# Grouped-query attention decode with token mixing: chunks of 4 MB in a ring of two, no V chunk kept over the layers, four V tiles in one matmul

## The chip, the cores and the metric

The kernel runs on one core of one Trainium2 chip. The metric is the device time of one execution in microseconds, as the median of several runs. Before the change it is 2613.38 us (3 runs, 2611.53 to 2614.95).

## What is computed

Two layers, each an attention block over a cached K and V and then a small MLP over the token axis. There are 2 sequences (B) with one new token each, 32 query heads on 8 K/V heads, 32768 cached positions (Sk) and heads of 128 (Dh). All is float32. Both layers read the same caches and weights. K and V hold 268 MB each, so two layers read 1074 MB of them.

```python
def _A_ref(x, k_cache, v_cache, wq, wo):
    q = (x @ wq).reshape(B, Sq, Hq, Dh).transpose(0, 2, 1, 3)
    k = jnp.repeat(k_cache, rep, axis=1)
    v = jnp.repeat(v_cache, rep, axis=1)
    scores = jnp.einsum("bhqd,bhkd->bhqk", q, k) * (Dh ** -0.5)
    p = _softmax(scores, axis=-1)
    o = jnp.einsum("bhqk,bhkd->bhqd", p, v)
    return o.transpose(0, 2, 1, 3).reshape(B, Sq, Hq * Dh) @ wo
...
def _B_ref(x, w1, b1, w2, b2):
    h = _layernorm(x, axis=-1)
    u = jnp.einsum("bsd,sf->bdf", h, w1) + b1
    u = _gelu(u)
    y = jnp.einsum("bdf,fs->bds", u, w2) + b2
    return y.transpose(0, 2, 1)
...
x = x + _A_ref(_layernorm(x, axis=-1), A_k_cache, A_v_cache, A_wq, A_wo)
x = x + _B_ref(_layernorm(x, axis=-1), B_w1, B_b1, B_w2, B_b2)
x = x + _A_ref(_layernorm(x, axis=-1), A_k_cache, A_v_cache, A_wq, A_wo)
x = x + _B_ref(_layernorm(x, axis=-1), B_w1, B_b1, B_w2, B_b2)
```

## The kernel before

The work is cut into 32 units: 2 layers times 2 sequences times 8 K/V heads. A unit has 8 K chunks and 8 V chunks (`NCH`) of 4096 positions (`CK`), 2 MB each: 128 rows of 16 KB. The host lays K out transposed, so that a chunk has Dh on the partitions; a V chunk has 32 positions on each partition, one V tile (`j`) of 128 columns for each of them.

All chunks go through one ring of three tiles (`chunk`, L53, L168 and L237), and all their DMAs are issued on SyncE's queue (SP), in the order of the program. A DMA into a ring tile waits until the matmuls that read the tile's last content are done. The first V chunk of the last K/V head is different: with `KEEP` = 1 it is loaded once into a tile of its own (L233) and used in both layers.

`k_chunk` (L165) multiplies the chunk by the four queries of the group. `qpad` has the queries in a window of zeros, so that each matmul adds its scores in other rows of the same PSUM tile: 128 x 32 stationary, 512 columns moving, on one of four column groups of TensorE (`g`). `SUB` windows for each chunk and `PACK` chunks fill one PSUM tile; VectorE then transposes it by blocks into `S` (L189) and takes maxima (L190). `max_1` and `max_2` (L199, L207) bring the maximum of the unit to all partitions, and ScalarE takes the exponentials and their sums (L217).

`v_chunk` (L228) multiplies each V tile by its four columns of `S`, one matmul of 128 columns each, into one PSUM accumulator, four rows in each of four column groups. `out_1` (L257) copies the accumulator, adds the groups up with a selection matrix (`selg`) and divides by the sum; `out_2` (L268) multiplies by wo. After the last head of a sequence comes the mixer: `mix_2` (layer norms), `mix_3` (VectorE and GELU on ScalarE, in four pieces of 2, 4, 4 and 4 tiles of 512), `mix_3_out` (TensorE) and `mix_4`. In the very last mixer, the pieces of `mix_3` use ring tiles (L301).

The order of the work on each engine is that of the program (`manual_schedule`). A list of slots (L343 to L393) sets it: in slot s the K chunk s is issued and multiplied, then come the `pre` steps, then V chunk s - NCH - LAG, then the `post` steps. The small steps of a unit (`make_q`, the loads of wq and wo, `max_1`, `out_1` and the mixer) are put in slots by hand. The last V chunk of the kernel is loaded in pieces of 16, 8, 4 and 4 tiles (`PIECES`).

Of the kernel before, what the change touches and what calls it, by code (L numbers as in the profile page):

```python
# [8 lines left out]
F32 = mybir.dt.float32  # L9
# [4 lines left out]
P = 128  # L14
CK = 4096
JT = CK // P
NG = 4
SUB = 2
PACK = 4
RING = 3  # L20
LAG = 1
KEEP = 1
PIECES = (16, 8, 4, 4)
GELU_GROUPS = (2, 4, 4, 4)
# [4 lines left out]
def gqa_mixer_kernel(ctx: ExitStack, tc: tile.TileContext, x, kt, v, wq, wo, cols, out):  # L29
# [19 lines left out]
    SCALE = DH ** -0.5  # L49
    assert DH == P and R * PACK * SUB == 32 and DT == NG and R == NG and D == 512  # L50

# [20 lines left out]
    def load_wo(h):  # L72
# [16 lines left out]

    selg = const.tile([P, R], F32, name="selg")  # L90
    nc.vector.tensor_reduce(
        selg, ident.rearrange("p (g r) -> p r g", g=NG)[:, :R, :], axis=AX.X, op=ALU.add
    )
# [6 lines left out]
    for t in acc:  # L100
        nc.vector.memset(t[:, :DH], 0.0)
    rows = pfix.tile([P, 512], F32, name="rows")
# [125 lines left out]
    def v_chunk(n, c):  # L228
# [14 lines left out]
        half, i = divmod(c, PACK)  # L243
        a = acc[n % 2]
        for j in range(JT):
            g = j % NG
            k, jj = divmod(j, JT // SUB)
            col = jj * 32 + (SUB * i + k) * R
            nc.tensor.matmul(  # L249
                a[32 * g : 32 * g + R, :DH],  # L250
                S[n][:, half, col : col + R],
                vc[:, j * DH : (j + 1) * DH],
                start=(c == 0 and j < NG),
                stop=(c == NCH - 1 and j >= JT - NG),
            )

    def out_1(n):  # L257
        asb = work.tile([P, DH], F32, name="asb", bufs=1)
        nc.vector.tensor_copy(asb, acc[n % 2][:, :DH])
        po = pmisc.tile([P, 512], F32, name="misc")  # L260
        nc.tensor.matmul(po[:, R : 2 * R], ones, lsum[n], start=True, stop=True)  # L261
        nc.tensor.matmul(po[:, :R], asb, selg, start=True, stop=True)  # L262
# [85 lines left out]
    for n in range(NU):  # L348
        layer, b, h = unit_of(n)
        s0 = n * NCH  # L350
        if n:
            at(post, s0 - 4, make_q, n, 0)
            at(pre, s0 - 3, make_q, n, 1)
            at(post, s0 - 3, make_q, n, 2)
            at(pre, s0 - 2, make_q, n, 3)
        if n and n < HKV:
            at(post, s0 - 6, load_wq, h)
        if n < HKV:
            at(post, s0 + NCH + 2, load_wo, h)
        at(pre, s0 + NCH, max_1, n)  # L360
        at(post, s0 + NCH, max_2, n)
        e = s0 + 2 * NCH + LAG
        at(pre, e, out_1, n)
        at(post, e, out_2, n)
        if h == HKV - 1:
            key = (layer, b)
            at(post, e, take_rows, key)
            at(pre, e + 1, mix_2, key)
            for k, w in enumerate(GELU_GROUPS):
                at(pre, e + 2 + k, mix_3, key, sum(GELU_GROUPS[:k]), w)  # L370
                at(post, e + 2 + k, mix_3_out, key, sum(GELU_GROUPS[:k]), w)
            at(post, e + 5, take_rows, key)
            at(pre, e + 6, mix_4, key)
            if layer + 1 < LAYERS:
                at(pre, e + 7, lambda k: to_columns(k, hx[k]), (layer + 1, b))

# [19 lines left out]
def _layout(A_x, A_k_cache, A_v_cache, A_wq, A_wo, B_w1, B_b1, B_w2, B_b2):  # L396
# [7 lines left out]

    kt = A_k_cache.reshape(B * HKV, n, NG, 32, SUB, JT // SUB, DH).transpose(0, 1, 6, 4, 2, 5, 3)
    wq = A_wq.reshape(D // P, P, HKV, -1).transpose(2, 1, 0, 3)
# [35 lines left out]
```

## Time and profile before

| | |
|---|---|
| median of 3 runs | 2613.38 us |
| the profiled execution, its time | 2613.11 us |
| its span, first to last instruction | 2611.3 us |
| mean granted clock of TensorE | 0.786 |
| HBM read | 1088.45 MB |
| chunk DMAs, K / V, from issue to landing (median) | 11.9 / 12.1 us |

PE is TensorE's matmuls and PEld its weight loads, DVE is VectorE, ACT ScalarE, POOL GpSimd. SP is SyncE; SPq is its queue, on which it issues DMAs. In the rows of the timeline stand start and duration in us, engine, line and operation, the tiles written and read, the number of instructions taken together, and in brackets the idle time before them and what ended it. In the rows of groups, the count is followed by busy time in us, the mean of one in ns, and the idle time before them with its cause. In the rows of stretches stand, after the length, busy time and count for PE, PEld, DVE, ACT and POOL, then the granted clock of TensorE (1.00 is full speed), the busy share of the DMA engines and GB/s. The queues' rows give packets, MB and the share of the time of 16 DMA engines.

### The profile page before, as it was taken

Reading aid. Unit: us, or ns where it says so; the run is one execution under the profiler, and the core shown is the slowest. Engines: PE = TensorE matmul, PEld = TensorE weight load, DVE = VectorE, ACT = ScalarE, POOL = GpSimd, SP = SyncE. Lnnn points to the kernel's source line nnn. Section 1 sums busy time; section 2 is a strip of 40 time slices with the busy share of each in tenths; the row PEclk is TensorE's granted clock in tenths of the full one; section 3 lists DMA queues with packets and bytes.
Section 4 is the critical chain, followed back from the end, with each engine's and each line's share of the span. In section 5 each row is a group of like instructions: output and inputs, shape, how many; then the busy total and the mean of one; then the engine's idle time right before and its main releaser. Section 6 shows DMA issues by size and latency. Waiting matters only on the chain.

```text
span 2611.3 us, 46425 instructions
## 1 busy us (share of the span) xinstructions
PE 1640.0 (63%) x22184; PEld 838.7 (32%) x22184; DVE 210.7 (8%) x473; ACT 135.3 (5%) x280; POOL 7.0 (0%) x21
## 2 busy tenths in 40 slices
PE   6556656566566666666666656656657666566665
PEld 3323323233333332332333333333323333233322
DVE  1000000000021000000002000000001100000002
ACT  0000000000010000000001000000000100000001
POOL 0000000000000000000000000000000000000000
PEclk8777777777888787887878888788787877877777
DMA  9999999999999999999999999999999999999995
GB/s 405 426 426 425 419 425 422 424 422 426 420 426 420 425 423 421 424 423 424 426 421 425 422 424 422 423 424 424 420 426 422 424 423 423 424 425 419 426 424 230
DMA packets 76660, 1091.44 MB, mean 418 GB/s; under 512 B 8628, under 2 KB 8628, under 8 KB 9016
## 3 DMA queue, kind: packets, MB, share of 16 engines
q1 hardware_dynamic: 76324, 1088.46, 98.8%
q8 instruction: 173, 2.83, 0.4%
q14 instruction: 15, 0.12, 0.0%
q10 hardware_dynamic: 148, 0.03, 0.0%
HBM read 1088.45 MB, written 0.00 MB: 417 GB/s over the span
## 4 chain that ended last, share of the span: by engine, by line
DMA 79%; PE 19%; issue 1%; DVE 0%; ACT 0%; SPq 0%; POOL 0%; POOLq 0%; DVEq 0%; ACTq 0%
DMA chunk<-in_kt_dram 40%; DMA chunk<-in_v_dram 40%; PE scores L178 9%; PE acc L249 9%; PE misc L153 0%; PE rows L322 0%; DVE chunk L307 0%; PE misc L132 0%; ACT chunk L315 0%; PE bcast L290 0%; ACT S L217 0%; DVE ln_st L110 0%; DVE row L114 0%; PE rows L271 0%; PE bcast L291 0%
## 5 line engine op out<-in xcount | busy, mean ns | idle before, releaser
L249 PE MATMUL acc<-chunk,S 128*4 128x128 f32 x16256 | 702.3, 344 | 478.5 <-DMA chunk<-in_v_dram 477.9
L178 PE MATMUL scores<-chunk,qpad 128*32 128x512 f32 x4096 | 678.8, 795 | 465.4 <-DMA chunk<-in_kt_dram 464.9
L249 PEld LDWEIGHTS acc<-chunk,S 128*4 128x4 f32 x16256 | 499.9, 105 | 767.4 <-DMA chunk<-in_v_dram 605.4
L178 PEld LDWEIGHTS scores<-chunk,qpad 128*32 128x32 f32 x4096 | 132.4, 128 | 783.0 <-DMA chunk<-in_kt_dram 410.5
L217 ACT ACTIVATE S<-S,neg 128x256 f32<-128x256 f32 x128 | 95.3, 749 | 2286.2 <-DVE neg L213 2286.2
L153 PEld LDWEIGHTS misc<-xnT,wq 128*128 128x128 f32 x1024 | 143.3, 217 | 97.3 <-issue 97.3
L153 PE MATMUL misc<-xnT,wq 128*128 128x1 f32 x1024 | 153.8, 272 | 0.0
L189 DVE STREAM_TRANSPOSE S<-scores 128x512 f32<-128x512 f32 x64 | 45.9, 717 | 899.1 <-PE scores L178 899.1
L161 DVE COPY qpad<-misc 128x4 f32<-128x4 f32 x32 | 5.2, 163 | 795.9 <-PE misc L153 795.9
L190 DVE TENSOR_REDUCE mx<-S 128x4 f32<-128x512 f32 x64 | 67.8, 1059 | 2.2
L271 PE MATMUL rows<-wo,oT 128*1 128x512 f32 x256 | 38.8, 679 | 0.5 <-DVE oT L266 0.5
L205 DVE TENSOR_REDUCE m<-misc 4x1 f32<-4x128 f32 x32 | 8.9, 279 | 230.0 <-PE misc L203 230.0
L315 ACT ACTIVATE hid<-hid 128x2048 f32<-128x2048 f32 (+1 forms) x12 | 20.4, 1697 | 130.0 <-DVE hid L307 130.0
L307 DVE TENSOR_SCALAR hid<-row,cols_sb 128x512 f32<-128x512 f32 x42 | 20.2, 542 | 58.6 <-PE rows L322 58.6
L217 ACT ACTIVATION_READ_ACCUMULATOR S<-S,neg 128x1 f32 x128 | 23.9, 187 | 0.0
L261 PEld LDWEIGHTS misc<-lsum,one 128*128 128x128 f32 x64 | 10.9, 214 | 37.0 <-issue 36.9
L264 DVE RECIPROCAL rl<-misc 128x4 f32<-128x4 f32 x32 | 5.9, 183 | 142.8 <-PE misc L262 142.8
L213 DVE TENSOR_SCALAR neg<-misc 128x4 f32<-128x4 f32 x32 | 5.2, 162 | 149.4 <-PE misc L209 149.4
L203 PEld LDWEIGHTS misc<-ident,mxa 128*4 128x4 f32 x64 | 6.4, 102 | 27.5 <-issue 26.6
L322 PE MATMUL rows<-hid,cols_sb 128*1 128x512 f32 x84 | 14.5, 688 | 1.2 <-ACT hid L315 1.2
L203 PE MATMUL misc<-ident,mxa 128*4 128x128 f32 x64 | 14.5, 314 | 0.8 <-DVE mxa L201 0.8
L209 PEld LDWEIGHTS misc<-ident,m 4*128 4x128 f32 x64 | 11.5, 222 | 10.8 <-issue 10.2
(50 smaller groups left out, 189.6 us busy)
## 6 DMA issues: line engine op xcount, KB each, us to landing
chunk<-in_kt_dram SPq DMA_DIRECT2D x256, 2048.0 KB, 11.9
chunk<-in_v_dram SPq DMA_DIRECT2D x253, 2048.0 KB, 12.1
wq<-in_wq_dram SPq DMA_DIRECT2D x8, 1024.0 KB, 16.0
wo<-in_wo_dram SPq DMA_DIRECT2D x8, 1024.0 KB, 13.4
kept<-in_v_dram SPq DMA_DIRECT2D x1, 2048.0 KB, 15.9
chunk<-in_v_dram SPq DMA_DIRECT2D x1, 1024.0 KB
chunk<-in_v_dram SPq DMA_DIRECT2D x1, 512.0 KB, 9.9
chunk<-in_v_dram SPq DMA_DIRECT2D x2, 256.0 KB, 10.2
```

The costliest lines, as they stand in the source:

```text
L153: nc.tensor.matmul(q_ps[n][:, r : r + 1], wq_sb[h][:, d, r * DH : (r + 1) * DH], xnT[layer, b][:, d : d + 1], start=(d == 0), stop=(d == D ...
L178: nc.tensor.matmul(sc_ps[n][32 * g : 32 * g + 32, :], q, kc[:, (k * NG + g) * w : (k * NG + g + 1) * w], start=(i == 0 and k == 0), stop=( ...
L189: nc.vector.transpose(S[n][:, half, :], sc_ps[n])
L190: nc.vector.tensor_reduce(mx[n][:, half, :], S[n][:, half, :].rearrange("p (t h) -> p h t", h=R), axis=AX.X, op=ALU.max,)
L203: nc.tensor.matmul(pm[:R, :P], mxa, ident, start=True, stop=True)
L209: nc.tensor.matmul(pm[:, :R], m4[n].to_broadcast([R, P]), ident[:R, :R], start=True, stop=True)
L217: nc.scalar.activation(s[:, :, h], s[:, :, h], AF.Exp, bias=neg[:, h : h + 1], scale=SCALE, accum_out=lsum[n][:, h : h + 1],)
L249: nc.tensor.matmul(a[32 * g : 32 * g + R, :DH], S[n][:, half, col : col + R], vc[:, j * DH : (j + 1) * DH], start=(c == 0 and j < NG), sto ...
L271: nc.tensor.matmul(rows[32 * r : 32 * r + 1, :], oT[n][:, r : r + 1], wo_sb[h][:, r, :], start=(h == 0), stop=(h == HKV - 1),)
L307: nc.vector.tensor_scalar(u[:, k * D : (k + 1) * D], hx[key], w1c[:, f : f + 1], b1c[:, f : f + 1], op0=ALU.mult, op1=ALU.add,)
L315: nc.scalar.activation(u[:, : n * D], u[:, : n * D], AF.Gelu_apprx_tanh)
L322: nc.tensor.matmul(rows[32 * g : 32 * g + 1, :], w2c[:, f : f + 1], u[:, k * D : (k + 1) * D], start=(f < NG), stop=(f >= FT - NG),)
```

## The change

A chunk is twice as large (8192 positions, 4 MB, rows of 32 KB), the ring has two tiles, and no V chunk is kept. A unit has 4 K and 4 V chunks, so there are half as many slots and the steps in the slots are moved. In `v_chunk` one matmul takes four V tiles: 512 columns moving, and as stationary the 16 columns of `S` that belong to the four tiles. Of its 16 x 512 results only the blocks where tile and columns belong together are used: `out_1` copies the whole accumulator and picks the blocks with four matmuls. The host lays K out so that the 16 columns stand side by side. The last V chunk has one more piece, of 32 tiles, ahead of the others. Each piece of the mixer is put in the slots next to the `mix_3_out` of the piece before it.

```diff
-CK = 4096
+CK = 8192
 JT = CK // P
 NG = 4
-SUB = 2
-PACK = 4
-RING = 3
+SUB = 4
+PACK = 2
+RING = 2
 LAG = 1
-KEEP = 1
-PIECES = (16, 8, 4, 4)
+KEEP = 0
+PIECES = (32, 16, 8, 4, 4)
+QT = 4
...
-    selg = const.tile([P, R], F32, name="selg")
+    selg = const.tile([P, R * QT], F32, name="selg")
...
-        a = acc[n % 2]
-        for j in range(JT):
-            g = j % NG
-            k, jj = divmod(j, JT // SUB)
-            col = jj * 32 + (SUB * i + k) * R
-            nc.tensor.matmul(
-                a[32 * g : 32 * g + R, :DH],
-                S[n][:, half, col : col + R],
-                vc[:, j * DH : (j + 1) * DH],
-                start=(c == 0 and j < NG),
-                stop=(c == NCH - 1 and j >= JT - NG),
-            )
+        w = QT * DH
+        a, c2 = divmod(i, PACK // 2)
+        for q in range(JT // QT):
+            g = q % NG
+            col = (c2 * (JT // QT) + q) * 32 + a * R * QT
+            nc.tensor.matmul(
+                acc[n % 2][32 * g : 32 * g + R * QT, :],
+                S[n][:, half, col : col + R * QT],
+                vc[:, q * w : (q + 1) * w],
+                start=(c == 0 and q < NG),
+                stop=(c == NCH - 1 and q >= JT // QT - NG),
+            )
...
-        asb = work.tile([P, DH], F32, name="asb", bufs=1)
-        nc.vector.tensor_copy(asb, acc[n % 2][:, :DH])
+        asb = work.tile([P, QT * DH], F32, name="asb", bufs=1)
+        nc.vector.tensor_copy(asb, acc[n % 2])
...
-        nc.tensor.matmul(po[:, :R], asb, selg, start=True, stop=True)
+        for t in range(QT):
+            nc.tensor.matmul(
+                po[:, :R],
+                asb[:, t * DH : (t + 1) * DH],
+                selg[:, t * R : (t + 1) * R],
+                start=(t == 0),
+                stop=(t == QT - 1),
+            )
...
-            at(post, s0 - 4, make_q, n, 0)
-            at(pre, s0 - 3, make_q, n, 1)
-            at(post, s0 - 3, make_q, n, 2)
-            at(pre, s0 - 2, make_q, n, 3)
+            at(post, s0 - 3, make_q, n, 0)
+            at(pre, s0 - 2, make_q, n, 1)
+            at(post, s0 - 2, make_q, n, 2)
+            at(pre, s0 - 1, make_q, n, 3)
         if n and n < HKV:
-            at(post, s0 - 6, load_wq, h)
+            at(post, s0 - 4, load_wq, h)
         if n < HKV:
-            at(post, s0 + NCH + 2, load_wo, h)
+            at(post, s0 + NCH + 1, load_wo, h)
...
+            places = [(post, e + 1), (pre, e + 2), (post, e + 2), (pre, e + 3), (post, e + 3)]
             for k, w in enumerate(GELU_GROUPS):
-                at(pre, e + 2 + k, mix_3, key, sum(GELU_GROUPS[:k]), w)
-                at(post, e + 2 + k, mix_3_out, key, sum(GELU_GROUPS[:k]), w)
-            at(post, e + 5, take_rows, key)
-            at(pre, e + 6, mix_4, key)
+                f0 = sum(GELU_GROUPS[:k])
+                at(*places[k], mix_3, key, f0, w)
+                at(*places[k + 1], mix_3_out, key, f0, w)
+            at(post, e + 3, take_rows, key)
+            at(pre, e + 4, mix_4, key)
             if layer + 1 < LAYERS:
-                at(pre, e + 7, lambda k: to_columns(k, hx[k]), (layer + 1, b))
+                at(pre, e + 5, lambda k: to_columns(k, hx[k]), (layer + 1, b))
...
-    kt = A_k_cache.reshape(B * HKV, n, NG, 32, SUB, JT // SUB, DH).transpose(0, 1, 6, 4, 2, 5, 3)
+    kt = A_k_cache.reshape(B * HKV, n // PACK, 2, PACK // 2, NG, 32, JT // QT, QT // SUB, SUB, DH)
+    kt = kt.transpose(0, 1, 2, 7, 9, 8, 4, 3, 6, 5)
```

More of the change, by code (lines that the diff above doesn't have):

```diff
@@ L49, in gqa_mixer_kernel @@
     SCALE = DH ** -0.5
-    assert DH == P and R * PACK * SUB == 32 and DT == NG and R == NG and D == 512
+    assert DH == P and R * PACK * SUB == 32 and PACK * SUB == 2 * QT and DT == NG and R == NG and D == 512
     const = ctx.enter_context(tc.tile_pool(name="const", bufs=1))
@@ L88, in gqa_mixer_kernel @@
     nc.gpsimd.memset(half_neg, -0.5)
-    selg = const.tile([P, R], F32, name="selg")
+    selg = const.tile([P, R * QT], F32, name="selg")
     nc.vector.tensor_reduce(
-        selg, ident.rearrange("p (g r) -> p r g", g=NG)[:, :R, :], axis=AX.X, op=ALU.add
+        selg, ident.rearrange("p (g r) -> p r g", g=NG)[:, : R * QT, :], axis=AX.X, op=ALU.add
     )
@@ L100, in gqa_mixer_kernel @@
     for t in acc:
-        nc.vector.memset(t[:, :DH], 0.0)
+        nc.vector.memset(t, 0.0)
     rows = pfix.tile([P, 512], F32, name="rows")
```

## The prediction

> **What bounds the kernel now.** I read the page of the profile first: busy time by engine, the 40 slices, the queues, the chain that ended last.
>
> ```profile
> span 2611.3 us, 46425 instructions
> PE 1640.0 (63%) x22184; PEld 838.7 (32%) x22184; DVE 210.7 (8%) x473; ACT 135.3 (5%) x280; POOL 7.0 (0%) x21
> DMA  9999999999999999999999999999999999999995
> GB/s 405 426 426 425 419 425 422 424 422 426 420 426 420 425 423 421 424 423 424 426 421 425 422 424 422 423 424 424 420 426 422 424 423 423 424 425 419 426 424 230
> DMA packets 76660, 1091.44 MB, mean 418 GB/s; under 512 B 8628, under 2 KB 8628, under 8 KB 9016
> q1 hardware_dynamic: 76324, 1088.46, 98.8%
> q8 instruction: 173, 2.83, 0.4%
> DMA 79%; PE 19%; issue 1%; DVE 0%; ACT 0%; SPq 0%; POOL 0%; POOLq 0%; DVEq 0%; ACTq 0%
> ```
>
> No compute engine is near full, while the 16 DMA engines are busy in every slice but the last. Slices 2 to 39 average 423.4 GB/s (38 figures of the fifth line), and the best reach 426. So the kernel streams bytes, with a head (405 in the first slice) and a tail (230 in the last). The chain's "PE 19%" need not contradict this, so I looked at the chain in order of time and at the timeline of a quiet stretch.
>
> ```profile
> 842.07 12.68 DMA chunk<-in_v_dram
> 856.78 12.68 DMA chunk<-in_kt_dram
> ```
> ```profile
> 835.17 3.37 PE L249 MATMUL acc<-chunk,S 128*4 128x128 f32 x64 [3.30 <-DMA chunk<-in_v_dram]
> 838.58 0.33 SPq L169 DMA_DIRECT2D chunk<-in_kt_dram  x1
> 840.08 1.92 PE L178 MATMUL scores<-chunk,qpad 128*32 128x512 f32 x16 [1.54 <-DMA chunk<-in_kt_dram]
> 842.07 0.33 SPq L241 DMA_DIRECT2D chunk<-in_v_dram  x1
> ```
>
> One turn of the ring is 856.78 - 842.07 = 14.71 us for three chunks, 4.90 us for 2.097 MB (428 GB/s). Of these 12.68 go from issue to landing and 2.03 on PE. A chunk alone moves in 4.90, so at its issue 12.68 - 4.90 = 7.8 us of older transfers still stood in the queue. PE's time lies under that queue: it is on the chain because a ring closes through PE, but shorter matmuls would only lengthen the wait in the queue.
>
> **The change, part by part.**
>
> *Bytes.* KEEP = 0 loads the last unit's first V chunk in both layers: 2.097 MB more, at 423.4 GB/s +4.95 us. Nothing hides it, since the queue is full.
>
> *Four V tiles in one matmul.* The profile counts two matmuls and two weight loads for each call.
>
> ```profile
> L249 PE MATMUL acc<-chunk,S 128*4 128x128 f32 x16256 | 702.3, 344 | 478.5 <-DMA chunk<-in_v_dram 477.9
> L178 PE MATMUL scores<-chunk,qpad 128*32 128x512 f32 x4096 | 678.8, 795 | 465.4 <-DMA chunk<-in_kt_dram 464.9
> ```
> ```profile
> 2580.93 1.93 PE L249 MATMUL acc<-chunk,S 128*4 128x128 f32 x64 [1.56 <-DMA chunk<-in_v_dram]
> ```
> ```profile
> 40.12 3.62 PE L178 MATMUL scores<-chunk,qpad 128*32 128x512 f32 x16 [1.99 <-DMA chunk<-in_kt_dram]
> ```
> ```profile
> 835.00:840.00 5.00, 3.37 (x64) 2.38 (x64) 0.00 (x0) 0.00 (x0) 0.00 (x0) 0.66 1.01 433
> 840.00:845.00 5.00, 1.94 (x19) 0.43 (x21) 0.00 (x0) 0.00 (x0) 0.00 (x0) 1.00 0.99 423
> ```
>
> A V chunk now is 64 matmuls of 128 columns, later 16 of 512 for the same 2 MB: the same 8192 columns, the form a K chunk has already. At granted clock 1.00 both take 1.92 to 1.93 us, at a lower clock (0.66 over the V burst at 835) 3.37 to 3.62. So PE's time per byte stays, and a 4 MB chunk takes 2 x 1.92 = 3.84 us warm and about 2 x 3.5 = 7.0 slow. What falls is the count: 254 chunks x 64 stand in the row (256 with the two it lacks, 16,384), later 4,096, each with its weight load, so 24,576 instructions go; out_1's three more calls in each of 32 units add 384. That is 24,192 of 46,425, or 52%, and the instruction queue shrinks with them. By bytes, 1.47 MB at 423.4 GB/s is 3.5 us; by its 0.4% of the span (10.4 us), 5.4. I take -4.5, from rows on both sides.
>
> *DMAs of 4 MB.* Some 260 DMAs and half of the small packets go. No row prices a DMA by itself. The bounds are 0 and, if that fixed work is all that keeps the average slice at 423.4 below 426, 0.6% of 2580 = -16 us. I take 0: neighbouring slices of one kernel differ by more (419 beside 425), so the dips are not a cost of each DMA.
>
> *The ring of two.* This is the term that decides.
>
> ```profile
> 1.43 0.62 SPq L65 DMA_DIRECT2D xrow<-in_x_dram  x2
> 3.37 0.69 DVE L110 BATCH_NORM_STATS2 ln_st<-xrow 128x6 f32<-128x512 f32 x1 [0.89 <-DMA xrow<-in_x_dram]
> ```
>
> After a landing, PE works 3.84 to 7.0 us, SP issues (0.04 us behind PE: 835.17 + 3.37, then 838.58), and the transfer starts. The two 2 KB transfers bound that start: 3.37 - 1.43 = 1.9 us at most, landing included. Meanwhile one chunk is under way, 2 x 4.90 = 9.8 us. The margin is 9.8 - 3.84 - 1.9 = 4.1 us warm and 0.9 slow; before, with two chunks of 4.90 behind the landed one, it was 6.0 to 4.3. So a quiet chunk does not run dry. But the margin holds for the slowest of 16 DMA engines, and they need not be level: 173 instruction fetches at 0.4% x 16 x 2611.3 / 173 = 0.97 us each fall on single engines (16 KB in one packet), so an engine can be two fetches, 1.9 us, behind the others. Those in front then wait where the margin is below that. Bounds: 0, and 83 remaining fetches each paid in full, 80 us. The margin covers two to four fetches unless the clock is slow, so I take one in twenty, +4.
>
> The Trainium skill, TensorE: Matmul & The Clock Gate, section Why this matters for your kernels, speaks against the change: a PE pause above about 3 us puts the clock back to half. With bursts 9.8 us apart the pause would be up to 6 us, against 1.5 to 3.3 in the rows above, which already show clocks of 0.66. By that rule every chunk starts slow and the margin lies nearer 0.9 than 4.1; the sum keeps its +4, and the dry ring below gets a higher chance.
>
> *Steps moved between slots.* A slot is now a K and a V chunk of 4 MB, 19.6 us in place of 9.8, so each make_q, max and GELU piece has as much time per chunk as before or more. wq and wo loads stay on SP between chunk issues and wait for nothing. One step collides: out_1 now follows the K chunk whose scores are transposed (an odd chunk with PACK 2), so PE waits there for DVE.
>
> ```profile
> L189 DVE STREAM_TRANSPOSE S<-scores 128x512 f32<-128x512 f32 x64 | 45.9, 717 | 899.1 <-PE scores L178 899.1
> L190 DVE TENSOR_REDUCE mx<-S 128x4 f32<-128x512 f32 x64 | 67.8, 1059 | 2.2
> ```
>
> That is 0.72 + 1.06, then the copy of acc (0.69) and four pairs of 0.39, in all 4.0 us behind K's 3.84 to 7.0, against 9.8 to V's landing. I cost it at nothing: V's transfer is the cover. Slow, it makes V 1.2 us late, 32 x 1.2 = 38 us at most if no margin is left.
>
> *Head and tail.* At the head, the queue holds wq, K, wq, K (10.5 MB, 25 us) while PE does the first chunk: 0. In the tail nothing is hidden.
>
> ```profile
> 2586.18 0.40 PE L249 MATMUL acc<-chunk,S 128*4 128x128 f32 x8 [0.24 <-DMA chunk<-in_v_dram]
> ...
> 2586.65 0.29 DVE L259 COPY asb<-acc 128x128 f32<-128x128 f32 x1 [32.55 <-PE acc L249]
> ...
> 2587.00 0.39 PE L262 MATMUL misc<-selg,asb 128*128 128x4 f32 x2
> ...
> 2588.96 0.69 DVE L283 COPY row<-rows 128x512 f32<-128x512 f32 x1 [1.16 <-PE rows L271]
> ...
> 2601.23 0.10 PEld L322 LDWEIGHTS rows<-chunk,cols_sb 128*1 128x1 f32 x8 [1.71 <-ACT chunk L315]
> 2601.45 1.92 DVE L307 TENSOR_SCALAR chunk<-row,cols_sb 128x512 f32<-128x512 f32 x4 [0.84 <-PE rows L322]
> 2603.03 0.10 PEld L322 LDWEIGHTS rows<-chunk,cols_sb 128*1 128x1 f32 x8 [1.70 <-ACT chunk L315]
> 2603.49 1.91 ACT L315 ACTIVATE chunk<-chunk 128x2048 f32<-128x2048 f32 x1 [0.50 <-DVE chunk L307]
> 2605.45 1.04 PE L322 MATMUL rows<-chunk,cols_sb 128*1 128x512 f32 x8 [1.13 <-ACT chunk L315]
> ...
> 2607.38 1.12 PE L334 MATMUL bcast<-row,selg 128*128 128x512 f32 x2 [0.89 <-DVE row L283]
> ```
>
> The last piece: one call of 512 columns, 1.12 as at L334, for 0.40 (+0.7). The copy of acc: 0.69, as L283 copies 512 columns from PSUM, for 0.29 (+0.4). Three more pairs of 0.39, partly overlapped (+1.0). The last GELU pieces take ring buffers, now two: the third piece must wait for the first one's matmuls, as the fourth did (DVE at 2601.45), so it takes the fourth's place on DVE (to 2603.4) and ACT (to 2605.4), and the fourth ends one ACT pass, 1.9 us, later. In all +4.0; bounds +2 (the matmuls overlap, the pieces do not shift) and +5.
>
> **The sum.** 2611.3 + 4.95 - 4.5 + 0 + 4 + 4.0 = 2619.8 us of span. The profiled run took 2613.1, so 1.8 lie around the span, and it is 0.3 below the median of 2613.38: 2619.8 + 1.8 + 0.3 = 2622 us, 0.3% slower. The terms are small beside the bytes, and of both signs.
>
> **The rivals.**
>
> *Large rows stream faster* (not slower). If the 4 MB DMAs hold every slice at 426 GB/s, the stream loses 16 us: 2622 - 16 = 2606. For it: half as many DMAs, packets and instruction fetches. Against it: 426 is reached today with 16 KB rows, and the dips have no rhythm of chunks. It decides from an average of 425 GB/s upwards, where the stream is 9 us shorter.
>
> The Trainium skill, DMA: Bandwidth & Descriptors, section Anatomy of one DMA, fits a DMA as 2.0 us fixed plus its bytes at 436 GB/s; 256 DMAs fewer would by that be 512 us, an estimate of some 2110. The ring's turn of 14.71 us for three chunks leaves no such gaps, because queued DMAs overlap, and I give that outcome no chance.
>
> *The ring covers all of it.* The lag of DMA engines costs 0 and the tail +4: 2618, 0.17% slower, not told from no change. For it: the margin of 4.1 when warm. Against it: the clocks of 0.66.
>
> *The ring runs dry.* Chunks at half clock leave 0.9 us, and every engine's lag, and every late V behind out_1, goes through to the stream. Price: half of the 80 for the fetches and a quarter of the 38, 40 + 10 = 50 us, 2622 - 4 + 50 = 2668. For it: pauses above those of today. Against it: a burst that starts slow need not end slow (1.93 for a V chunk at 2580.93, behind a pause).
>
> *The change does not do what it says*: PE's 1640 us hardly fall, because the columns stream as before. That holds in each case and costs nothing, as PE is not the bound.
>
> **How the numbers follow.** Forecast 0.45 (2619 to 2632), covered ring 0.22 (2613 to 2618.6), faster stream 0.21, dry ring 0.12. No change means within 0.2%, 2608.2 to 2618.6, about what a measurement of this kernel can tell. Slower: 0.45 + 0.12 = 0.57, plus a little of the edge, 0.58; same 0.22 less the edge, 0.21; faster 0.21. The range reaches from 2604, just beyond the faster case's price, to 2648, half way into the dry ring's 2632 to 2668.
>
> **What would show it.** Right: q8 near 83 packets and 1.4 MB; acc matmuls 4,096 of 512 columns at about the K row's mean; chunk DMAs of 4096 KB landing in 19.6 - 6 = some 13 to 15 us; slices still 421 to 425 GB/s; a tail 4 us longer between the last landing and the end. Wrong: slices at 426 and above throughout (fast rival), or slices under 420 with PE waits of more than the 9.8 us of a transfer (dry ring), or a PE burst of a chunk under 3.8 us. The forecast falls if the mean rate of the middle slices moves by more than 1% either way.

## The result, and the profile after

The changed kernel takes 2689.37 us (median of 4 runs, 2677.4 to 2692.84) against 2613.93 before on the same chip: a ratio of 1.0282, 95% interval 1.0249 to 1.0315. It is slower by 75 us, where the prediction had 2622 and a range of 2604 to 2648. The profiled execution took 2688.18 us, its span is 2686.4.

The page of the changed kernel, the lines that answer to those of before:

```profile
span 2686.4 us, 21703 instructions
PE 1675.4 (62%) x10088; PEld 522.9 (19%) x10088; DVE 219.5 (8%) x473; ACT 133.5 (5%) x280; POOL 7.0 (0%) x21
GB/s 408 420 420 425 413 418 421 421 399 416 402 413 400 417 409 416 405 410 409 413 411 407 405 419 412 404 414 405 411 411 408 409 417 405 413 406 418 404 411 212
DMA packets 39986, 1091.95 MB, mean 406 GB/s; under 512 B 4564, under 2 KB 4564, under 8 KB 4952
q1 hardware_dynamic: 39748, 1090.54, 97.4%
q8 instruction: 79, 1.29, 0.2%
DMA 71%; PE 27%; DVE 1%; issue 0%; ACT 0%; SPq 0%; POOL 0%; POOLq 0%; DVEq 0%; ACTq 0%
L180 PE MATMUL scores<-chunk,qpad 128*32 128x512 f32 x4096 | 699.4, 846 | 509.2 <-DMA chunk<-in_kt_dram 509.2
L253 PE MATMUL acc<-chunk,S 128*16 128x512 f32 x4096 | 712.7, 859 | 399.1 <-DMA chunk<-in_v_dram 399.1
chunk<-in_kt_dram SPq DMA_DIRECT2D x128, 4096.0 KB, 15.0
```

Nothing was added on PE: it is busy 1675 us, where it was 1640, with less than half the matmuls, and the instruction queue fell from 173 packets to 79. What changed is the stream: slices 2 to 39 average 411.5 GB/s (before 423.4), and none of them reaches 426. Nearly the whole loss is there: the 1050 MB of these slices at 411.5 in place of 423.4 take 72 us longer. The stream is lower nearly everywhere (399 to 425), which points at a cause in each turn of the ring and not in a few places. In the chain PE's share rose from 19% to 27%.

The next view is the timeline of the changed kernel in a stretch without a mixer, PE's bursts on a chunk and SP's issues alone:

```profile
1007.54 5.32 PE L253 MATMUL acc<-chunk,S 128*16 128x512 f32 x32 [0.45 <-DMA chunk<-in_v_dram]
1012.92 0.33 SPq L243 DMA_DIRECT2D chunk<-in_v_dram  x1
1017.29 3.64 PE L180 MATMUL scores<-chunk,qpad 128*32 128x512 f32 x32 [2.58 <-DMA chunk<-in_kt_dram]
1020.99 0.33 SPq L171 DMA_DIRECT2D chunk<-in_kt_dram  x1
1027.26 6.29 PE L253 MATMUL acc<-chunk,S 128*16 128x512 f32 x32 [5.34 <-DMA chunk<-in_v_dram]
1033.62 0.33 SPq L243 DMA_DIRECT2D chunk<-in_v_dram  x1
1036.97 6.56 PE L180 MATMUL scores<-chunk,qpad 128*32 128x512 f32 x32 [2.44 <-DMA chunk<-in_kt_dram]
1043.60 0.33 SPq L171 DMA_DIRECT2D chunk<-in_kt_dram  x1
```

Each issue follows its burst at once, and the bursts are long: 5.3, 3.6, 6.3, 6.6 us. Over the kernel the two rows of groups give (699.4 + 712.7) / 256 = 5.5 us for each of 256 chunks. The prediction's margin, the transfer of the other chunk less the burst and less the start, is then 9.75 (4.19 MB at 430 GB/s) - 5.5 - 1.9 = 2.3 us on the average, and 1.3 behind a burst of 6.6. The 3.64 us at 1017.29 are a warm burst (granted clock 1.00). Stretches of 1 us in the changed kernel show why the others are longer (columns as in the profile before; the last three are the granted clock, the DMA share and GB/s):

```profile
834.00:835.00 1.00, 1.00 (x8) 0.20 (x4) 0.00 (x0) 0.00 (x0) 0.00 (x0) 0.50 0.91 393
...
837.00:838.00 1.00, 1.00 (x12) 0.29 (x8) 0.00 (x0) 0.00 (x0) 0.00 (x0) 0.50 0.91 393
838.00:839.00 1.00, 1.00 (x16) 0.22 (x8) 0.00 (x0) 0.00 (x0) 0.00 (x0) 0.95 0.99 426
...
849.00:850.00 1.00, 1.00 (x8) 0.17 (x4) 0.00 (x0) 0.00 (x0) 0.00 (x0) 0.50 0.99 426
850.00:851.00 1.00, 1.00 (x8) 0.17 (x4) 0.00 (x0) 0.00 (x0) 0.00 (x0) 0.50 0.48 197
851.00:852.00 1.00, 1.00 (x12) 0.28 (x8) 0.00 (x0) 0.00 (x0) 0.00 (x0) 0.62 0.08 33
852.00:853.00 1.00, 1.00 (x16) 0.19 (x8) 0.00 (x0) 0.00 (x0) 0.00 (x0) 1.00 0.00 0
```

A burst began at 833.6 after 6.6 us without matmuls. For its first four microseconds the clock is 0.50 and 8 to 12 matmul instructions pass in each; then it is at full speed and 16 pass. A shorter pause can do it too: the burst at 1036.97 above ran at 0.50 for five microseconds, after 2.44 us of idle time behind 1.05 us of one-column matmuls. The second part, in a mixer, shows the extreme: PE is still at the chunk that landed first (its burst began only at 846.86, behind `out_1` and the mixer's layer norm), the other one has landed, nothing is queued, and the DMA engines stand still until SP issues. That is the dry ring to be seen with the eye. Most turns lose far less than this one: 411.5 against 430.6 GB/s (the first experiment's rate) is 0.45 us for each chunk of 4.19 MB.

### The profile page after: what moved, and what is told of

Read it like the earlier page. It is cut to its first block, busy times and chain, and to the rows that moved or that the text cites. A ratio compares the mean times of both kernels' runs of the same rounds, so it can differ in the third digit from the quotient of the medians.

```text
span 2686.4 us, 21703 instructions
## 1 busy us (share of the span) xinstructions
PE 1675.4 (62%) x10088; PEld 522.9 (19%) x10088; DVE 219.5 (8%) x473; ACT 133.5 (5%) x280; POOL 7.0 (0%) x21
## 4 chain that ended last, share of the span: by engine, by line
DMA 71%; PE 27%; DVE 1%; issue 0%; ACT 0%; SPq 0%; POOL 0%; POOLq 0%; DVEq 0%; ACTq 0%
DMA chunk<-in_kt_dram 70%; PE scores L180 26%; DMA chunk<-in_v_dram 2%; PE acc L253 1%; PE misc L267 0%; DVE chunk L318 0%; ACT chunk L326 0%; PE rows L333 0%; DVE ln_st L112 0%; PE rows L282 0%; DVE row L116 0%; DVE xrow L347 0%; DVE mx L192 0%; PE bcast L345 0%; DVE asb L263 0%
## 5 line engine op out<-in xcount | busy, mean ns | idle before, releaser
L180 PE MATMUL scores<-chunk,qpad 128*32 128x512 f32 x4096 | 699.4, 846 | 509.2 <-DMA chunk<-in_kt_dram 509.2
L253 PE MATMUL acc<-chunk,S 128*16 128x512 f32 x4096 | 712.7, 859 | 399.1 <-DMA chunk<-in_v_dram 399.1
L180 PEld LDWEIGHTS scores<-chunk,qpad 128*32 128x32 f32 x4096 | 166.4, 148 | 961.7 <-issue 585.5
L253 PEld LDWEIGHTS acc<-chunk,S 128*16 128x16 f32 x4096 | 141.9, 126 | 868.4 <-issue 471.7
L155 PEld LDWEIGHTS misc<-xnT,wq 128*128 128x128 f32 x1024 | 127.2, 195 | 105.3 <-issue 105.3
L155 PE MATMUL misc<-xnT,wq 128*128 128x1 f32 x1024 | 137.0, 255 | 0.0
L267 PE MATMUL misc<-selg,asb 128*128 128x4 f32 x256 | 47.3, 308 | 73.7 <-DVE asb L263 73.7
L267 PEld LDWEIGHTS misc<-selg,asb 128*128 128x128 f32 x256 | 44.5, 262 | 76.5 <-DVE asb L263 76.5
L263 DVE COPY asb<-acc 128x512 f32<-128x512 f32 x32 | 21.8, 681 | 33.2 <-PE acc L253 33.2
L333 PE MATMUL rows<-chunk,cols_sb 128*1 128x512 f32 x28 | 6.6, 909 | 11.8 <-ACT chunk L326 11.8
## 6 DMA issues: line engine op xcount, KB each, us to landing
chunk<-in_v_dram SPq DMA_DIRECT2D x127, 4096.0 KB, 14.7
chunk<-in_v_dram SPq DMA_DIRECT2D x2, 256.0 KB, 14.7
```

The source lines that it names most:

```text
L155: nc.tensor.matmul(q_ps[n][:, r : r + 1], wq_sb[h][:, d, r * DH : (r + 1) * DH], xnT[layer, b][:, d : d + 1], start=(d == 0), stop=(d == D ...
L180: nc.tensor.matmul(sc_ps[n][32 * g : 32 * g + 32, :], q, kc[:, (k * NG + g) * w : (k * NG + g + 1) * w], start=(i == 0 and k == 0), stop=( ...
L253: nc.tensor.matmul(acc[n % 2][32 * g : 32 * g + R * QT, :], S[n][:, half, col : col + R * QT], vc[:, q * w : (q + 1) * w], start=(c == 0 a ...
L263: nc.vector.tensor_copy(asb, acc[n % 2])
L267: nc.tensor.matmul(po[:, :R], asb[:, t * DH : (t + 1) * DH], selg[:, t * R : (t + 1) * R], start=(t == 0), stop=(t == QT - 1),)
```

## The experiments

Three explanations were set against each other. Theory A: the ring of two closes too late, because the burst leaves too little of the other chunk's transfer. B: DMAs of 4 MB with rows of 32 KB are slower in themselves. C: `out_1`, now behind the transposes, makes PE wait and delays the next chunk. The time of before is 2612.9 us in all of them, and ratios are to it.

### Half of the matmuls

Half of the chunk matmuls are left out, so scores and weighted sums cover half of the positions; all bytes are loaded.

```diff
-        for k in range(SUB):
+        for k in range(SUB // 2):
...
-        for q in range(JT // QT):
+        for q in range(JT // QT // 2):
```

> The changed kernel with half of its chunk matmuls left out: of the four windows of queries in a K chunk the last two, and of the 16 calls in a V chunk the last eight. DMAs, ring and slots stay as they are. Theory A (the ring closes too late: PE's burst of about 6 us leaves too little of the 9.8 us of one transfer): the burst halves, the margin grows by about 3 us, the slices go back to 421-425 GB/s and the time to 2605-2625 us. Theory B (4 MB DMAs with rows of 32 KB are slower by themselves): 2675-2695 us. Theory C (single late bursts, behind out_1's wait for DVE and in the mixer, make all of the loss): the waits for DVE stay, 2640-2680 us.

Measured: 2570.3 us, ratio 0.9837 (0.9823 to 0.985), lower than any theory had. The page of this kernel:

```profile
GB/s 408 432 432 431 431 429 430 431 431 431 431 430 431 432 425 431 430 431 431 432 431 429 429 430 431 430 431 431 430 432 432 430 430 430 428 432 432 431 432 214
L180 PE MATMUL scores<-chunk,qpad 128*32 128x512 f32 x2048 | 456.8, 1042 | 685.4 <-DMA chunk<-in_kt_dram 685.4
L253 PE MATMUL acc<-chunk,S 128*16 128x512 f32 x2048 | 453.3, 1036 | 537.1 <-DMA chunk<-in_v_dram 537.1
```

The same DMAs and the same ring now hold 430.6 GB/s, more than the kernel before ever reached. So 4-MB transfers aren't slow in themselves; it is PE's burst, (456.8 + 453.3) / 256 = 3.55 us here, that decides. B falls as a reason for the loss.

### Three quarters of the matmuls

As above with three quarters, a point between.

```diff
-        for k in range(SUB):
+        for k in range(SUB * 3 // 4):
...
-        for q in range(JT // QT):
+        for q in range(JT // QT * 3 // 4):
```

> The changed kernel with a quarter of its chunk matmuls left out (three of four windows of queries in a K chunk, 12 of 16 calls in a V chunk). Theory A: burst of about 4.8 us in place of 6 (whole) and 3.4 (half), so between 2570 and 2689 and nearer to the half: 2585-2635 us, with slices mixed between 410 and 430 GB/s. If the loss came from the amount of PE's reading as such, half way: about 2630.

Measured: 2608.4 us (2599.03 to 2622.75, 10 runs), ratio 0.9987 (0.9969 to 1.0005), under the 2630 of a loss that goes by the amount of PE's reading. The groups of its bursts:

```profile
L180 PE MATMUL scores<-chunk,qpad 128*32 128x512 f32 x3072 | 615.3, 964 | 578.5 <-DMA chunk<-in_kt_dram 578.5
L253 PE MATMUL acc<-chunk,S 128*16 128x512 f32 x3072 | 612.3, 961 | 425.4 <-DMA chunk<-in_v_dram 425.3
```

The bursts take (615.3 + 612.3) / 256 = 4.8 us and slices 2 to 39 average 423.9. So the loss of rate against the 430.6 of the first experiment grows with the burst: 1.6% at 4.8 us (a margin of 3.0 by the formula above), 4.4% at 5.5 (2.3), where 3.55 leaves 4.3. It starts while there is still a margin of 3 us on the average.

### Each chunk in two DMAs, and the late start

The first kernel loads every chunk in two DMAs of 2 MB (rows of 16 KB).

```diff
-        nc.sync.dma_start(kc, kt[b * HKV + h, c])
+        for part in (slice(0, CK // 2), slice(CK // 2, CK)):
+            nc.sync.dma_start(kc[:, part], kt[b * HKV + h, c, :, part])
...
-            for k in PIECES if n == NU - 1 and c == NCH - 1 else (JT,):
+            for k in PIECES if n == NU - 1 and c == NCH - 1 else (JT // 2, JT // 2):
```

> The changed kernel, but each 4 MB chunk is loaded by two DMAs of 2 MB with rows of 16 KB, issued one behind the other when the tile is free. Theory A: the tile comes free at the same moment, so 2675-2700 us. Theory B: rows and DMAs are those of before, so 2612-2630 us. Theory C as A.

Measured: 2600.1 us, ratio 0.9949 (0.9936 to 0.9963). What theory A was made to expect here was a misjudgement of the edit, as the timeline of this kernel shows:

```profile
1004.95 1.92 PE L181 MATMUL scores<-chunk,qpad 128*32 128x512 f32 x16 [0.74 <-DMA chunk<-in_kt_dram]
1009.84 3.42 PE L181 MATMUL scores<-chunk,qpad 128*32 128x512 f32 x16 [2.97 <-DMA chunk<-in_kt_dram]
1013.18 1.05 PE L155 MATMUL misc<-xnT,wq 128*128 128x1 f32 x8
1013.33 0.80 SPq L172 DMA_DIRECT2D chunk<-in_kt_dram  x2
```

PE takes the first half 4.9 us before the second lands, so only 3.4 us of work stand between the last landing and the next issue. The edit changed the burst as well as the DMAs. The second kernel takes that apart: the same two DMAs, but each burst begins with the half that lands last.

```diff
+        ks = [(k + SUB // 2) % SUB for k in range(SUB)]
-        for k in range(SUB):
+        for k in ks:
...
-        for q in range(JT // QT):
+        for o in range(JT // QT):
+            last = n == NU - 1 and c == NCH - 1
+            q = o if last else (o + JT // QT // 2) % (JT // QT)
```

> As e2 (each 4 MB chunk by two DMAs of 16 KB rows), but PE multiplies the second half of a chunk first, so that its burst starts only when the whole chunk has landed, as in the changed kernel (the last V chunk keeps its order). Theory A (the ring closes too late; e2 helped because PE worked on the first half while the second was still under way): the burst behind the landing is whole again, about 6 us, so 2660-2700 us. Theory B (one DMA of 4 MB with rows of 32 KB starts or runs badly): as e2, 2598-2612 us.

Measured: 2688.9 us, ratio 1.0289 (1.0274 to 1.0305): all of the gain is gone, with the same DMAs, bytes and matmuls, only their order turned round. This is theory A's clearest evidence. Split transfers don't help; an early start of PE does. Nor do they cost anything that can be measured: 512 chunk DMAs of 2 MB here and 256 of 4 MB in the changed kernel give 2688.9 and 2689.4 us.

### `out_1` moved

```diff
-        at(pre, e, out_1, n)
+        at(post, e - 1, out_1, n)
```

> The changed kernel with out_1 one step earlier, right behind the unit's last V chunk, ahead of the K chunk whose scores VectorE transposes. It takes away PE's waits for the copy of acc (73.7 us in 32 places in the changed kernel), no more than 4.6 us each. Theory A alone (every burst is late): 2660-2690 us. Theory C (these 32 places carry the loss): 2610-2640 us.

Measured: 2688.7 us, ratio 1.0283 (1.0259 to 1.0308), as without the edit. The group of `out_1`'s matmuls, first in the changed kernel, then with the move:

```profile
L267 PE MATMUL misc<-selg,asb 128*128 128x4 f32 x256 | 47.3, 308 | 73.7 <-DVE asb L263 73.7
```
```profile
L267 PE MATMUL misc<-selg,asb 128*128 128x4 f32 x256 | 33.8, 255 | 17.9 <-DVE asb L263 17.9
```

PE's wait for the copy falls from 73.7 to 17.9 us and the time stays. C falls: the prediction's 0 for this step was right as far as runs that spread by 15 us can tell.

### The clock: matmuls of zeros between the bursts

If a burst is long because it starts at half clock, work on PE in the pause should make the kernel faster. The matmuls added have an all-zero stationary and go into the accumulator, which they leave as it is. First three of them behind six of eight bursts:

```diff
+    def keep_busy(s):
+        t = s - NCH - LAG
+        if 0 <= t < NU * NCH and t % NCH:
+            for _ in range(3):
+                nc.tensor.matmul(
+                    acc[t // NCH % 2],
+                    zero,
+                    wq_sb[0].rearrange("p t c -> p (t c)")[:, :512],
+                    start=False,
+                    stop=False,
+                    skip_group_check=True,
+                )
```

> The changed kernel with three matmuls of zero weights (128 x 512, added to the accumulator, which they do not change) behind six of eight chunk bursts, to keep TensorE's clock up through the pause. If the bursts are long because they start at half clock, they shrink from about 6 us to 3.8-4.5, and the ring closes as early as in e6 or e1: 2575-2615 us. If the clock is not what makes the ring late: 2680-2700 us.

Measured: 2647.6 us, ratio 1.0138 (1.0117 to 1.0159), 42 us less by useless matmuls that take 526 us of PE (1110 in the profile, two for each call), but between the two ranges named. The timeline of this kernel:

```profile
1005.60 5.32 PE L269 MATMUL acc<-chunk,S 128*16 128x512 f32 x32 [3.07 <-DMA chunk<-in_v_dram]
1010.85 2.84 PE L235 MATMUL acc<-wq,zero 128*128 128x512 f32 x6
...
1015.32 3.64 PE L180 MATMUL scores<-chunk,qpad 128*32 128x512 f32 x32 [0.84 <-DMA chunk<-in_kt_dram]
1018.89 2.84 PE L235 MATMUL acc<-wq,zero 128*128 128x512 f32 x6
```

Here every other burst is warm; over the kernel 47% of the bursts take less than 4 us (9% in the changed kernel), and a warm one is mostly followed by a slow one. That fits a short burst that closes its tile early, so that the pause behind it is the longer. The mean burst, (597.9 + 615.0) / 256 = 4.7 us, is that of the kernel with three quarters, yet the time is 39 us longer: every fifth burst still takes more than 6 us, and there none does. That points at the late bursts rather than the mean. With `out_1` moved as well:

> e9 and e10 together: the 4 MB ring with warm bursts and out_1 out of the way. If both help, the stream reaches the 430 GB/s that rows of 32 KB had in e1, 1092 MB in 2540 us and head and tail of 33: 2572-2600 us, which may be under e4's 2592. If only the clock matters, as e9.

Measured: 2642.6 us, ratio 1.0105 (1.0088 to 1.0122); so it is as with the clock alone; the intervals of the two overlap, and the move's worth stays unclear. Then four and five such matmuls behind every burst, and `out_1` moved (the edit for five against the kernel with three):

```diff
-        if 0 <= t < NU * NCH and t % NCH:
-            for _ in range(3):
+        if 0 <= t < NU * NCH:
+            for z in range(5):
...
-                    start=False,
+                    start=(t % NCH == 0 and z == 0),
```

> After the change, with four matmuls whose stationary is all zeros behind every burst of chunk matmuls (the first of a unit's V accumulation included), and out_1 moved one chunk earlier. In e9 three such matmuls behind three of four V chunks left every other burst slow (5.32 us beside 3.64). Theory A (what is lost is the margin behind a landing, and the slow clock at the start of a burst eats it): if the bursts now reach 3.7 us each way, as e1's 3.55 did, the middle slices are at 427 to 431 GB/s and the time is 2575 to 2600 us. Rival (the ring of two loses time whatever the clock, by SP's issue and the start of the transfer): 2630 to 2645 us with bursts of 3.7 us.

> As the run with four zero matmuls, with five. The five take 2 us or more behind each burst. Theory A: bursts at 3.7 us and the time 2575 to 2600 us; if four are too few to keep the clock and five are enough, this run is the faster of the two by 10 us or more. Rival: 2630 to 2645 us, no faster than with four.

Measured: 2611.2 us (ratio 1.0002, 0.9986 to 1.0017) with four, between the two ranges, and 2603.6 us (0.9965, 0.9953 to 0.9977) with five. The page, the timeline and the stretches of the second:

```profile
PE 2324.1 (89%) x12548; PEld 897.0 (34%) x12548; DVE 222.8 (9%) x473; ACT 137.3 (5%) x280; POOL 7.1 (0%) x22
GB/s 399 430 429 429 432 423 424 423 426 430 424 426 400 425 430 426 431 430 427 431 428 426 392 432 431 429 430 428 428 427 433 421 416 429 432 429 429 431 425 197
L180 PE MATMUL scores<-chunk,qpad 128*32 128x512 f32 x4096 | 510.7, 643 | 126.5 <-DMA chunk<-in_kt_dram 126.5
L269 PE MATMUL acc<-chunk,S 128*16 128x512 f32 x4096 | 480.5, 609 | 118.1 <-DMA chunk<-in_v_dram 118.1
```
```profile
1004.84 3.63 PE L269 MATMUL acc<-chunk,S 128*16 128x512 f32 x32 [0.42 <-DMA chunk<-in_v_dram]
...
1014.56 3.64 PE L180 MATMUL scores<-chunk,qpad 128*32 128x512 f32 x32 [0.82 <-DMA chunk<-in_kt_dram]
```
```profile
810.00:820.00 10.00, 8.90 (x43) 3.85 (x42) 1.72 (x5) 1.08 (x3) 0.00 (x0) 0.95 0.95 387
820.00:830.00 10.00, 10.00 (x48) 3.36 (x44) 2.45 (x3) 2.00 (x6) 0.00 (x0) 0.88 0.68 270
```

The bursts are down to (510.7 + 480.5) / 256 = 3.87 us (87% of them under 4 us), and with the changed kernel's own ring of two and its own DMAs the stream runs at 428 GB/s and above in 22 of slices 2 to 39, where it never passed 425. The time ends 4 us above what theory A named. The two worst slices, 400 and 392, are at mixers: there the zero matmuls queue behind each other with the mixer's own work, PE is busy 10.00 of 10 us, and the stream falls to 270 GB/s. (430 - 387 + 430 - 270) / 430 x 10 us are 4.7 us for this mixer alone, as much as the miss. The rival (a ring of two loses whatever the clock) had 2630 to 2645 and falls. PE reads more here than in the changed kernel while the stream is faster, so PE's reading as such isn't what slows it.

### The parts alone

The kernel before with four V tiles in one matmul as the only edit (chunks of 2 MB, ring of three, V chunk kept); then the changed kernel with chunks of 2 MB in a ring of four, and the steps in the slots of before.

```diff
+QT = 4
...
-        for j in range(JT):
+        for q in range(JT // QT):
...
-                vc[:, j * DH : (j + 1) * DH],
+                vc[:, q * w : (q + 1) * w],
```

> The kernel before with the four V tiles in one matmul alone (2 MB chunks, ring of three, V chunk kept). The prediction's terms: -4.5 us for 24,192 fewer instructions to fetch, +2.1 in the tail, 2613.9 - 2.4 = 2611.5 us, between 2607 and 2616. If instruction fetches delay single DMA engines by more than their own transfer (an engine that is 1 us late makes the chunk late), the gain is larger, to 2600 us.

```diff
-CK = 8192
+CK = 4096
...
-RING = 2
+RING = 4
```

> Chunks of 2 MB again, in a ring of four (the same 64 KB of each partition), with the four V tiles in one matmul, no kept V chunk and the slots of before. Three transfers of 4.9 us lie behind a landed chunk, 14.7 us against a burst of 1.9 to 3.5. Theories A, B and C alike: the stream is full again; 2613.9 + 4.95 (V chunk not kept) - 4.5 (instruction fetches) + 2.1 (tail without the shifted GELU piece) = 2616 us, 2611-2622. Over 2640 all three fall, and the four-tile matmul is to blame.

Measured: 2592.1 us (ratio 0.992, 0.9907 to 0.9934) and 2594.9 us (0.9931, 0.9917 to 0.9944). The first is the fastest complete kernel of this study and beats both of the kernels compared. Its page:

```profile
GB/s 404 428 427 427 427 426 427 427 427 424 427 428 426 425 427 428 427 424 426 428 427 426 427 428 426 424 427 428 422 428 428 428 419 428 428 428 428 427 428 211
q8 instruction: 79, 1.29, 0.2%
```

So four V tiles in one matmul are worth 20.7 us, where the prediction had about 4.5. Both kernels are faster than was expected of them, by 19 and 21 us, most of it this term. The bytes of the chunk no longer kept and a deeper ring together cost 2.8. And the changed kernel differs from the second by the size of the chunk and the depth of the ring (and the slots that follow from them) alone: 2689.4 - 2594.9 = 94.5 us. That is a net figure: what 4 MB DMAs gain, below, is already taken off.

Half of the matmuls in the first of the two (again half of the positions are left out) tells what the shorter burst does when the ring isn't short:

```diff
-        for k in range(SUB):
+        for k in range(SUB // 2):
...
-        for q in range(JT // QT):
+        for q in range(JT // QT // 2):
```

> The kernel of e4 (2 MB chunks, ring of three, four V tiles in one matmul) with half of its chunk matmuls left out. Theory R (the 431 GB/s of e1 come from rows of 32 KB): slices stay at 427-428 and the time at 2587-2593 us. Theory P (PE's reading of SBUF slows the transfers; e1 read half as much): slices go to 430-432, 2566-2576 us.

Measured: 2584.6 us, ratio 0.9891 (0.9876 to 0.9906), between the two ranges and near theory R's; slices mostly at 427 to 429, as R had it. That is 14.3 us above the changed kernel with half of the matmuls, which moves 2.1 MB (5 us) more: DMAs of 4 MB with rows of 32 KB do stream faster, by some 19 us over the kernel, once the ring leaves them room. The prediction's fast rival was right in that. Longer rows come with half as many DMAs and packets here, and no run takes the two apart.

### Where the 20 us of the four V tiles come from

Between the kernel before, the four V tiles alone and its half, the instruction queue has 173, 79 and 47 packets of 16 KB, and the time falls by 20.7 and then 7.5 us: 0.22 and 0.23 us for a packet. But TensorE's weight loads fall in the same steps, 22,184, 10,088 and 5,992, at 1.7 and 1.8 ns for each, and the second step also halves the chunk matmuls; so the counts fit a cost of weight loads just as well. To see whether instructions as such cost the stream, GpSimd was given idle work, memsets of a tile that nobody reads, for each V chunk: 64 and then 32 of one element on each partition, then 4 of 1024 elements, which keep it busy for about as long.

```diff
+    spare = const.tile([P, 1], F32, name="spare")
...
+        for _ in range(64):
+            nc.gpsimd.memset(spare, 0.0)
```

> The kernel of e4 with 64 small memsets on GpSimd beside each V chunk, 16,128 instructions more to fetch (63 packets of 16 KB) and nothing for TensorE. Theory F (the 20.7 us of e4 are instruction fetches: 94 fewer, 0.22 us each): 2592 + 14 = 2606 us, 2601-2611. Theory W (they are TensorE's 12,192 weight loads, which read SBUF beside the transfers): 2590-2596 us.

Measured: 2718.6 us, ratio 1.0405; it can't be read, since GpSimd itself became the bound at the end (half of the chain of waits). With 32:

> As e8 with 32 memsets beside each V chunk, so that GpSimd (0.16 us for each, 2580 us in e8) is done in half of the time and holds nothing up at the end. Theory F (instruction fetches, 0.23 us for each 256 instructions as from e4 to e7): 2592 + 8064 / 256 x 0.23 = 2599 us, 2596-2606. Theory W (weight loads of TensorE): 2590-2595 us. If memsets on GpSimd hold the transfers up in a way of their own, half of e8's loss of rate (415 against 427 GB/s): 2620-2635 us.

Measured: 2621.5 us, ratio 1.0032 (1.002 to 1.0044). Theory F's price is missed by a factor of four; the time lies in the third range, of memsets that hold the transfers up in a way of their own.

> e4 with 4 GpSimd memsets of 128 x 1024 for each V chunk, in place of e12's 32 of 128 x 1: GpSimd is as busy as in e12 at an eighth of the instructions. If e12's 29 us came from the fetching of instructions: 2594 to 2600 us. If they came from GpSimd's work itself (its writes to SBUF beside the transfers): 2615 us or more.

Measured: 2592.2 us, ratio 0.9921 (0.9903 to 0.9939), as without memsets. The pages of the run with 32 short memsets and of the one with 4 long ones:

```profile
POOL 6666600000035666400003666620000666650000
GB/s 404 423 416 418 410 421 427 428 427 424 427 428 427 419 409 416 411 426 428 428 428 427 421 418 414 413 412 428 427 428 424 428 420 417 412 415 426 428 428 226
q14 instruction: 79, 0.65, 0.1%
L247 POOL MEMSET spare<- 128x1 f32 x8192 | 816.1, 100 | 473.1
```
```profile
POOL 8999100000037998000004999500000999800000
GB/s 402 428 427 427 427 427 424 427 426 428 423 427 427 428 424 426 427 428 424 427 427 428 422 428 427 428 422 427 428 428 425 428 427 427 423 427 428 428 422 218
L247 POOL MEMSET spare<- 128x1024 f32 x1024 | 980.4, 957 | 58.4
```

In the first the stream drops in the slices where GpSimd is busy (mostly 409 to 421, beside 427 and 428). In the second GpSimd is busier there and writes far more, and no slice drops in that way. So on GpSimd it is the number of instructions that costs, not its time or the amount it writes: 29.3 us for 7168 of them, 4.1 ns each. How they cost it isn't shown. Their fetches, 79 - 23 = 56 packets of 8 KB more on queue q14, would have to cost 0.52 us each, more than twice the 0.22 above for packets of 16 KB; for a TensorE instruction, 20.7 us / 24,192 is 0.9 ns. So the two don't share one price, and whether TensorE's 20.7 us are its fetches, its weight loads or something else stays open.

## Why the prediction was wrong, and where it was right

**The ring of two** is the step that failed. It was put at +4 us; between the ring of four and the changed kernel lie 94.5. What came is the mechanism of its dry ring, which got 0.12 and 50 us, and the sign by which it wanted its forecast to fall: the mean rate of the middle slices moved by more than 1%, from 423.4 to 411.5 GB/s. Three things went wrong in the term.

First the burst. It took the margin of 4.1 us, with a warm burst of 3.84, as the rule and 0.9 as the exception. The two rows that it shows give the mean: (702.3 / 254 + 678.8 / 256) us for a V and a K chunk of 2 MB, so 5.4 for 4 MB, and a mean margin of 2.5. Measured are 5.5 and 2.3. The bursts did not grow colder to speak of by the change (mean granted clock 0.786 before, 0.751 after); its rival sentence "pauses above those of today" looked for the danger there. What the change did is to put twice the work between a landing and the next issue, under the same 9.8 us of queued transfers; the ring of four has 14.7 over half of the work.

Second the lag of the DMA engines. The prediction allowed an engine to be 1.9 us behind the others, and beside a mean margin of 2.5 that would have been a warning. The traces hold 16 landings for each chunk, as many as there are DMA engines: in the changed kernel the first and the last are 2.2 us apart in the median. From a reissue to the other chunk's last landing there are 4.6 us on the average, to its first landing 2.4, of which a start takes up to 1.9. So the first engines run out of work while the formula, which counts to the last landing, still shows a margin; "a quiet chunk does not run dry" did not ask for them.

Third the price. It let one fetch in twenty be paid; lost are 0.45 us for each of 256 chunks against the rate of the first experiment.

The Trainium skill, TensorE: Matmul & The Clock Gate, section Why this matters for your kernels, was quoted in the prediction as speaking against the change, and the trace agrees: after pauses of 5.3 and 6.6 us the clock is 0.50 for the first four microseconds of the burst and more. The same section asks for TensorE to be kept busy for about 4 us to reach full clock, which agrees with the 0.50 up to 838 in a burst begun at 833.6. The measured mean margin of 2.3 lies between the prediction's 4.1 and 0.9; the sum kept its +4, which went with the first.

**Instructions.** The count was right (24,192 predicted; 46,425 - 21,703 = 24,722), q8 too (79 packets for 83). The price was not: -4.5 against -20.7. It spread a fetch over 16 engines, 0.97 / 16 = 0.06 us; the time that went is 0.22 us for each fetch less. If a fetch, 16 KB in one packet, keeps one engine back and the chunk has landed only when the last engine is done, a fetch costs more than its share; that this is the reason, and not the weight loads that went too, is not shown.

**Large rows.** The 4 MB DMAs were put at 0 with a bound of -16; they are worth some -19 where the ring isn't dry, and nothing shows of it in the changed kernel, whose slices don't reach 426. The reason given, that dips have no rhythm of chunks, didn't bear on the best rate.

**Bytes, PE, `out_1`.** 2.1 MB more were read, as put. PE's time per byte nearly stayed (699.4 us for K where it was 678.8, 712.7 for V where 702.3 stood for 254 of 256 chunks), and the landing came as named, 15.0 us for 13 to 15. The wait behind `out_1` costs nothing that can be measured. `KEEP` was not run alone.

**The tail.** From the copy of the accumulator to the end it was 2611.3 - 2586.65 = 24.7 us, and is now, in the timeline of the changed kernel,

```profile
2656.94 0.69 DVE L263 COPY asb<-acc 128x512 f32<-128x512 f32 x1 [33.23 <-PE acc L253]
```

2686.4 - 2656.94 = 29.5: 4.8 longer, where the steps behind the copy were put at 3.3 of the 4.0. The mechanism was right (DVE's third piece, at 2672.80, waits for PE's matmuls on the first) and its size slightly low.

So three sizable effects stood behind a sum of small ones, two for the change (about -21, and -19 that never came to bear) and one against it, and the forecast of "terms small beside the bytes" missed all three.

That the first engine's margin sets the loss fits the kernels with a ring of two and one DMA for each chunk, nearly in order. In the table, counted from the traces of the profiled executions, a short turn is one in which the other chunk's first landing comes less than 1.9 us, the bound for a start, after the reissue.

| kernel | mean of slices 2 to 39, GB/s | short turns |
|---|---|---|
| changed kernel | 411.5 | 35% |
| `out_1` moved | 413.5 | 35% |
| three zero matmuls, `out_1` moved | 418.4 | 30% |
| three zero matmuls | 419.0 | 26% |
| three quarters of the matmuls | 423.9 | 9% |
| four zero matmuls, `out_1` moved | 424.8 | 13% |
| five zero matmuls, `out_1` moved | 426.1 | 9% |
| half of the matmuls | 430.6 | 0% |

What stays open: why the engines are that far apart, since no run changed their lag alone, and what the 20.7 us of the wider matmuls are. A ring of three chunks of 4 MB wasn't tried.

## What to carry to other kernels

The depth of a ring is measured in time behind a landing: transfer of what is still queued, less the whole burst at the clock that the trace shows, less issue and start, and what is left has to cover the lag between the first and the last DMA engine. In a ring of a given size, larger chunks in fewer tiles put more work behind each landing and leave less in the queue to cover it. Where the margin is short, let the consumer start on the first half of a chunk, or keep its clock up, before adding bytes to a transfer. And in a kernel bound by DMA, try fewer and larger instructions: they may pay in the stream though no engine is near full.

## What the runs showed of the hardware

Useless matmuls made a kernel faster: 1,230 of them (2,460 in the profile), 1121 us of PE, brought the changed kernel, with `out_1` moved, from 2689.4 to 2603.6 us, as the useful bursts fell from 5.5 to 3.87 us. With three in a pause 47% of the bursts took less than 4 us, with five 87%. 8,192 memsets of one element on each partition, on an engine with nothing else to do, cost a DMA-bound kernel 29 us, and an eighth as many, each a thousand times as large, cost none. The 16 landings of a 4 MB DMA were 2.2 us apart in the changed kernel. DMAs with rows of 32 KB reached 430 to 433 GB/s on one core, with rows of 16 KB 427 to 429.
